# Early gates on 384 tokens, another order of loads and pacing, and seven products for the last block, in an attention and SwiGLU kernel

## The chip, the cores and the metric

The kernel runs on one core of one Trainium2 chip. Its time is the device time of one execution in microseconds (us); where several executions are given, the median is the figure that counts. The profile covers one execution, taken by the hardware profiler; its span runs from the first to the last instruction of the core. The engines are PE (TensorE: matrix products and transposes), ACT (ScalarE), DVE (VectorE), POOL (GpSimd) and SP (SyncE, which only issues transfers here). A tile name such as `kn` or `pg` is the name that the kernel gives to a buffer.

## The reference

Attention over 8 batches, 8 heads, 576 positions and 64 elements per head, causal, with a window of 128 positions and a linear bias that depends on the head; then a gated feed-forward layer over all 8 × 576 = 4608 rows of 512.

```python
scores = scale * np.matmul(q, k.transpose(0, 1, 3, 2))
bias = slopes[:, None, None] * (-np.abs(rel).astype(np.float32))[None, :, :]
mask = (rel >= 0) & (rel < window)                      # window = 128
attn = softmax(np.where(mask, scores + bias[None], -1e9))
x = np.matmul(attn, v)                                  # to 4608 x 512
g = x @ w_gate                                          # 512 x 1536
val = x @ w_val                                         # 512 x 1536
out = (g * (1.0 / (1.0 + np.exp(-g))) * val) @ w_out    # 1536 x 512, out in f32
```

Inputs and output are f32 in HBM; inside, the products run on f16 operands with f32 sums.

## The kernel before

**Tiling.** The attention is cut into 36 units of 128 query rows. A "rank" r = 9 s + p counts them: s is one of four pairs of batches, p = 0 to 7 are the full tiles of the pair, and p = 8 takes the two rests of 64 rows. For each rank there is a load of k, of q and of v (128 KB each). Four consecutive tiles of a batch fill one block of 512 tokens of the feed-forward layer; so there are nine blocks, block 8 being made of the rests.

**Loads.** All of k, q, v and the weights come over POOL's queue, cast from f32 to f16 on the way, in an order written out by hand near the end of the kernel (`load_qk`, `load_v`, `load`, `load_w`; L624 to L646). The two weights of the feed-forward layer come in four column slices each (0 to 256, 256 to 512, 512 to 1024, 1024 to 1536), `wo_sb` in two halves behind rank 8. k and q land in a pool of five buffers each (`kn`, `qn`), and the next load into a buffer waits until it has been transposed. Ranks below 11 are transposed by PE (`transposed`, L201, result `pt`, then copied to `kT` and `qT`); later ones by transfers that SP issues (`transpose`).

**Attention.** `scores` multiplies q and k into `ps` (or `psc` for the tiles with combined masks), ACT takes the exponential (`ex`, `exc`), DVE multiplies by a mask that holds the bias and the window. `reg` (`m_reg`) is the usual mask, made at the start by eight exponentials on ACT; `msk` (`m_c`) are three more, made from it by the four copies of `make_masks` (L109 to L112), and first used by the tile p = 7. `weighted` multiplies by v into `av` and divides by the sum of the weights (`x`), `x_transposed` puts x into `xT` by PE (`px`).

**Feed-forward.** For each block n and each of the 12 slices m of 128 columns, `wide` makes `pg` (gate) and `pv` (value), four matmuls of 512 columns each (L368); ACT takes a tanh (`tt`, L379), DVE makes `uu` = (tt + 1) · pg (L381) and then `hT` = uu · pv (L385). The factor 0.5 that this leaves is put back when the projection is evacuated. `project` is the plain product of `hT` with `wo_sb` (12 matmuls of 512 columns for each of the four groups of 128 rows, L398). `strassen` does it for two groups of rows at a time with seven products of half size, 6 matmuls of 256 columns each (L477), which need sums of the weights (`T1` to `T4`, made by `weight_sums` while block 1 is worked on) and of `hT` (`sums`, four DVE instructions for each of the last three m). Block 0 is projected by `project`, blocks 1 to 7 by `strassen`, block 8 by `project` for three groups of rows and by `last_project` for the fourth, which splits its columns in two halves.

**Order.** `first_tiles` works on tiles 0 to 3 in an order written by hand on PE, DVE and ACT (`tc.manual_schedule`), and begins the gates and values of block 0 on the first 256 or 384 tokens (`begin`, which leaves an open sum in `early`; `wide` finishes it). `everything` then goes through the steps of the generator `ffn`, still by hand up to step 8 (`ALONE`); behind that, a scheduler sets each engine's order from the order in which the program issues its work. How many steps of `attention` are issued between two steps of `ffn` comes from `target`:

```python
target = base + max(0, step - ALONE) + max(0, step - 16) * (32 - b1 + ALONE) / (b1 - 16)
```

With `b1` = 24 the last factor is 2. Block 1 begins at step 24.

**PSUM.** `ps_f` has three buffers `gv` (gates and values) and one `po`; `ps_a` has four buffers, shared by scores, `av`, `px`, `pt`, the gates and values of m = 0 and 1 of block 0, and the projection of block 8.

Of the kernel before, what the change touches and what calls it, by code (L numbers as in the profile page):

```python
# [10 lines left out]
FP32 = mybir.dt.float32  # L11
# [6 lines left out]
WIN = 128  # L18
QK_DMA_FROM = 11
X_DMA_FROM = 24  # L20
ALONE = 8
MANUAL = "compute"
ET = mybir.EngineType
# [23 lines left out]
def kernel(  # L47
# [312 lines left out]
    def wide(n, m, which, c1=512):  # L360

        w, ms = wg_sb if which == "g" else wv_sb, slice(m * P, (m + 1) * P)
        ps, c0 = early.pop((n, m, which), (None, 0))
        if ps is None:
            pool, tag = (ps_a, "a") if (n, m, which) in OTHER else (ps_f, "gv")
            ps = pool.tile([P, 512], FP32, name="p" + which, tag=tag)
        for kb in range(NKB):
            nc.tensor.matmul(ps[:, c0:c1], w[:, kb, ms], xT[n][:, kb, c0:c1],  # L368
                             start=(kb == 0 and c0 == 0), stop=(kb == NKB - 1 and c1 == 512))
        if c1 < 512:  # L370
            early[(n, m, which)] = (ps, c1)
        return ps

    def gate_val(n, m):
        if n not in hT:
            hT[n] = hpool.tile([P, NMB, 512], FP16, name="hT", tag="hT")
        pg = wide(n, m, "g")
        tt = supool.tile([P, 512], FP16, name="tt", tag="tt")
        nc.scalar.activation(tt, pg, AF.Tanh, scale=0.5)  # L379
        uu = supool.tile([P, 512], FP16, name="uu", tag="uu")  # L380
        nc.vector.scalar_tensor_tensor(out=uu, in0=tt, scalar=one if (n, m) == PIN else 1.0, in1=pg,  # L381
                                       op0=ALU.add, op1=ALU.mult)
        yield
        pv = wide(n, m, "v")
        nc.vector.tensor_mul(hT[n][:, m, :], uu, pv)  # L385
        yield

    def rows_of(n, j):
        if n == 8:
            return [(0, 64, 2 * j * S + 512), (64, 128, (2 * j + 1) * S + 512)]  # L390
        return [(0, 128, n * S + j * P)]

    def project(n, j, pool, tag, bufs):
        po = pool.tile([P, DM], FP32, name="po", tag=tag, bufs=bufs)
        for m0 in range(0, NMB, 4):
            for i in range(m0, m0 + 4):
                m = NMB - 1 - i if n == 0 else i
                nc.tensor.matmul(po, hT[n][:, m, j * P:(j + 1) * P], wo_sb[:, m, :],  # L398
                                 start=(i == 0), stop=(i == NMB - 1))
            if m0 + 4 == NMB:  # L400
                osb = opool.tile([P, DM], FP32, name="osb", tag="osb")
                nc.scalar.mul(osb, po, 0.5)
                for p0, p1, r0 in rows_of(n, j):
                    nc.sync.dma_start(out[r0:r0 + p1 - p0, :], osb[p0:p1, :])
            yield

    def last_project(n, j):

        osb = opool.tile([P, DM], FP32, name="osb", tag="osb")
        for half in range(2):  # L410
            c = slice(half * DM // 2, (half + 1) * DM // 2)
            po = ps_a.tile([P, DM // 2], FP32, name="po", tag="a", bufs=4)
            for m in range(NMB):
                nc.tensor.matmul(po, hT[n][:, m, j * P:(j + 1) * P], wo_sb[:, m, c],
                                 start=(m == 0), stop=(m == NMB - 1))
            if half == 0:
                nc.scalar.mul(osb[:, c], po, 0.5)
            else:
                nc.vector.tensor_scalar_mul(osb[:, c], po, 0.5)
            for i, (p0, p1, r0) in enumerate(rows_of(n, j)):  # L420
                (nc.sync if i == 0 else nc.scalar).dma_start(out[r0:r0 + p1 - p0, c], osb[p0:p1, c])
            yield 1.5

# [37 lines left out]
    def strassen(n, t):  # L461

        h = hT[n]
        A11, A12 = h[:, 0:HM, 0:256], h[:, HM:NMB, 0:256]
        S1, A22 = h[:, 0:HM, 256:512], h[:, HM:NMB, 256:512]
        S2, S3, S4 = hsum[n]
        cols = slice(t * P, (t + 1) * P)
        po = ps_f.tile([P, 2, HC], FP32, name="po", tag="po", bufs=1)
        p2 = ps_a.tile([P, HC], FP32, name="p2", tag="a")
        top, low = (opool.tile([P, DM], FP32, name="osb", tag="osb") for _ in range(2))  # L470
        p1s = supool.tile([P, HC], FP32, name="p1s", tag="p1s", bufs=1)
        p5s = supool.tile([P, HC], FP32, name="p5s", tag="p5s", bufs=1)
        u2s = supool.tile([P, HC], FP32, name="u2s", tag="u2s", bufs=1)

        def product(dst, a, b, start=False):
            for m in range(HM):
                nc.tensor.matmul(dst, a[:, m, cols], b[:, m, :], start=(start and m == 0),  # L477
                                 stop=(m == HM - 1), skip_group_check=True)

        def half_plus(dst, a, b):  # L480
            nc.vector.scalar_tensor_tensor(out=dst, in0=a, scalar=0.5, in1=b,
                                           op0=ALU.mult, op1=ALU.add)

        X, Y = po[:, 0, :], po[:, 1, :]
        product(X, A11, B11, True)
# [12 lines left out]
        half_plus(low[:, HC:DM], X, p5s)  # L498
        yield
        product(Y, S4, B22)  # L500
        half_plus(top[:, HC:DM], Y, u2s)
        yield
        product(X, A22, T4)
        nc.scalar.mul(low[:, 0:HC], X, 0.5)
        for j, osb in ((t, top), (t + 2, low)):
            for p0, p1, r0 in rows_of(n, j):
                nc.sync.dma_start(out[r0:r0 + p1 - p0, :], osb[p0:p1, :])
        yield

    AT = {2, 3, *range(5, 10), *range(11, 18)}
# [1 line left out]
    def ffn():  # L514

        for n in range(NBLK):
            if n > 1:
                parts = chain(strassen(n - 1, 0), strassen(n - 1, 1))
            if n == 1:
                for j in range(PRE):  # L520
                    for _ in project(0, j, ps_f, "po", 1):
                        yield 1.0
            for m in range(NMB):
                for half, _ in enumerate(gate_val(n, m)):
                    yield 1.0
                    if n > 1 and 2 * m + half in AT:
                        next(parts)
                        yield 0.75
                if n == 1:
                    if m % 2 and PRE + m // 2 < 4:  # L530
                        for _ in project(0, PRE + m // 2, ps_f, "po", 1):
                            yield 1.0
                    if m in (2, 4, 6):
                        weight_sums(m // 2 - 1)
                if 0 < n < NBLK - 1 and m >= 9:
                    sums(n, m - 9)
            if n > 1:
                assert next(parts, None) is None
        for j in range(3):
            for _ in project(NBLK - 1, j, ps_a, "a", 4):  # L540
                yield 1.0
        yield from last_project(NBLK - 1, 3)


    loaded = done_t = 0
# [31 lines left out]
    def first_tiles():  # L577

        first_masks()
        transposes_to(need[0] + 1)  # L580
        for n, _ in enumerate(run(scores(0))):
            if n == 0:
                transposes_to(need[1])
        for i in range(FIRST):
            if i + 1 < FIRST:
                for n, _ in enumerate(run(scores(i + 1))):
                    if n == 0 and i + 2 < FIRST:
                        transposes_to(need[i + 2])
            weighted(i)

            if i >= 2:
                begin(4, i - 1)
            if i > 0:
                x_transposed(i - 1)
        begin(6, 2)
        begin(4, 3)
        x_transposed(FIRST - 1)
        begin(6, 3)

    def attention():  # L600
# [35 lines left out]
    load_qk(5, "q")  # L636
    load_w(512, 1024)
    load_qk(5, "k")
    load_v(5)
    load_w(1024, 1536)  # L640
    load(6)
    load(7)
    load(8)
    loaded = 9
# [22 lines left out]
    def everything():  # L667
# [3 lines left out]
        with tc.manual_schedule(engines=ENGINES[MANUAL]):  # L671
# [3 lines left out]
            while (at := next(steps)) < ALONE:  # L675
                if at == 2.0:
                    nc.scalar.copy(idm2, idm)
                if at == 5.0:
                    make_masks()
        for step in steps:  # L680

            b1 = 24 + 3 * PRE

# [2 lines left out]
                   else min(NBLK - 1, 2 + int((step + lead - 60) // 34.5)))  # L686
            if step < b1:

                target = base + max(0, step - ALONE) + max(0, step - 16) * (32 - b1 + ALONE) / (b1 - 16)
            elif step < 60:  # L690
                target = base + 32 + SECOND * 8 * (step - b1) / (60 - b1)
            else:
# [35 lines left out]
```

The softmax here doesn't subtract the row's maximum and nothing guards it: scores larger than these inputs give would overflow.

## Time and profile before

| | |
|---|---|
| median of 10 executions | 357.31 us (357.18 to 357.73) |
| profiled execution | 357.18 us |
| its span | 355.4 us, so 1.8 us lie around it |
| mean granted clock of TensorE | 0.998 |
| PE busy | 341.6 us, 96% |
| DVE busy | 272.9 us, 77% |
| ACT busy | 178.2 us, 50% |
| POOL busy | 106.7 us, 30% |

A page of the profile gives the busy time of the engines, then the span in 40 equal slices of some 8.9 us with the busy share in tenths, then the queues of transfers, the chain of work that ended last, and the costliest groups of instructions. A group's line has the source line, the engine, the operation, output and inputs by their names, partitions × elements, the count, busy time and mean duration. A timeline's line has the start, the duration of the group and its operation; in brackets stands how long the engine idled just before it, and what ended that. The matmuls' ends are modelled and overlap with the next start, so spacing, not the single duration, gives their cost.

### The profile page before, as it was taken

Reading aid. Unit: us, or ns where it says so; the run is one execution under the profiler, and the core shown is the slowest. Engines: PE = TensorE matmul, PEld = TensorE weight load, DVE = VectorE, ACT = ScalarE, POOL = GpSimd, SP = SyncE. Lnnn points to the kernel's source line nnn. Section 1 sums busy time; section 2 is a strip of 40 time slices with the busy share of each in tenths; the row PEclk is TensorE's granted clock in tenths of the full one; section 3 lists DMA queues with packets and bytes.
Section 4 is the critical chain, followed back from the end, with each engine's and each line's share of the span. In section 5 each row is a group of like instructions: output and inputs, shape, how many; then the busy total and the mean of one; then the engine's idle time right before and its main releaser. Section 6 shows DMA issues by size and latency. Waiting matters only on the chain.

```text
span 355.4 us, 7251 instructions
## 1 busy us (share of the span) xinstructions
PE 341.6 (96%) x2765; PEld 196.9 (55%) x2765; DVE 272.9 (77%) x595; ACT 178.2 (50%) x353; POOL 106.7 (30%) x132
## 2 busy tenths in 40 slices
PE   7898899999999999999999999999999999999995
PEld 4683454544456655565456655664666566556643
DVE  4858786997977799678986998789878965975540
ACT  4847585555555554555555555455444323332321
POOL 8964755444738354454400100000000000000000
PEclk9999999999999999999999999999999999999999
DMA  9999999999999999999996413311022101101114
GB/s 151 171 186 188 142 172 154 92 148 134 151 139 161 159 157 157 172 145 172 181 75 105 62 59 30 90 31 59 17 75 52 53 2 59 62 0 62 38 43 97
DMA packets 157763, 37.34 MB, mean 105 GB/s; under 512 B 147232, under 2 KB 153248, under 8 KB 157728
## 3 DMA queue, kind: packets, MB, share of 16 engines
q0 software_dynamic: 116224, 18.62, 82.1%
q1 hardware_dynamic: 41056, 17.97, 27.5%
q8 instruction: 21, 0.34, 0.4%
q10 hardware_dynamic: 448, 0.30, 0.3%
q14 instruction: 14, 0.11, 0.1%
HBM read 37.91 MB, written 9.44 MB: 133 GB/s over the span
## 4 chain that ended last, share of the span: by engine, by line
PE 74%; DVE 13%; ACT 5%; DMA 5%; issue 2%; POOL 0%; DVEq 0%; ACTq 0%
PE pg L368 21%; PE pv L368 21%; PE po L477 14%; PE av L319 4%; DMA qn<-in_q_dram 4%; PE ps L254 3%; PE po L398 3%; DVE hT L385 2%; DVE uu L381 2%; PE p L477 2%; DVE ex L263 2%; PE px L345 2%; ACT ex L259 2%; ACT exc L286 1%; PE pt L201 1%
## 5 line engine op out<-in xcount | busy, mean ns | idle before, releaser
L368 PE MATMUL pg<-xT,wg_sb 128*128 128x512 f16 (+2 forms) x464 | 116.4, 365 | 0.2 <-ACT xT L346 0.2
L368 PE MATMUL pv<-xT,wv_sb 128*128 128x512 f16 (+2 forms) x464 | 114.7, 365 | 1.6 <-DVE uu L381 1.6
L379 ACT ACTIVATE tt<-pg 128x512 f16<-128x512 f32 x108 | 65.1, 604 | 85.9 <-PE pg L368 82.5
L381 DVE SCALAR_TENSOR_TENSOR uu<-tt,pg 128x512 f16<-128x512 f16 x107 | 73.2, 684 | 38.0 <-ACT tt L379 37.6
L385 DVE TENSOR_TENSOR hT<-uu,pv 128x512 f16<-128x512 f16 x108 | 73.9, 684 | 6.1 <-PE pv L368 2.1
L368 PEld LDWEIGHTS <-wv_sb 128*128 128x128 f16 x464 | 42.7, 98 | 38.8 <-issue 3.1
L368 PEld LDWEIGHTS <-wg_sb 128*128 128x128 f16 x464 | 42.4, 98 | 35.1 <-issue 2.9
L259 ACT ACTIVATE ex<-ps 128x512 f16<-128x512 f32 x96 | 50.1, 606 | 9.9 <-PE ps L254 9.8
L168 POOL DMA_DIRECT2D va<-in_v_dram x40 | 34.1, 856 | 51.5 <-PE av L319 36.1
L174 POOL DMA_DIRECT2D qn<-in_q_dram x39 | 33.6, 863 | 26.4 <-DMA qT<-qn 20.0
L174 POOL DMA_DIRECT2D kn<-in_k_dram x39 | 33.2, 861 | 26.3 <-DMA kT<-kn 16.1
L477 PEld LDWEIGHTS <-hT 128*128 128x128 f16 x336 | 31.8, 98 | 15.4 <-issue 3.5
L263 DVE TENSOR_TENSOR ex<-ex,m_reg 128x1024 f16<-128x1024 f16 x48 | 32.6, 688 | 8.3 <-ACT ex L259 8.3
L477 PEld LDWEIGHTS <-S 128*128 128x128 f16 x252 | 23.9, 98 | 11.7 <-issue 2.9
L322 DVE TENSOR_TENSOR x<-av,rec 128x256 f16<-128x256 f32 x72 | 29.0, 421 | 0.6
L477 PE MATMUL po<-T,S 128*128 128x256 f16 x168 | 23.0, 273 | 0.6 <-ACT p5s L495 0.6
L477 PE MATMUL po<-T,hT 128*128 128x256 f16 x168 | 23.1, 272 | 0.4
L286 ACT ACTIVATE exc<-psc 128x512 f16<-128x512 f32 x40 | 21.5, 610 | 3.4 <-PE psc L282 3.4
L346 ACT COPY xT<-px 128x512 f16<-128x512 f16 x24 | 14.1, 586 | 15.4 <-PE px L345 15.3
L319 PEld LDWEIGHTS <-ex 128*128 128x128 f16 x384 | 18.3, 97 | 4.9 <-issue 0.7
L319 PE MATMUL av<-va,ex 128*128 128x65 f16 x384 | 20.4, 193 | 0.5
L398 PE MATMUL po<-wo_sb,hT 128*128 128x512 f16 x84 | 19.7, 379 | 0.0
(74 smaller groups left out, 290.0 us busy)
## 6 DMA issues: line engine op xcount, KB each, us to landing
out_dram<-osb SPq DMA_DIRECT2D x32, 256.0 KB, 2.4
va<-in_v_dram POOLq DMA_DIRECT2D x32, 128.0 KB, 8.5
qn<-in_q_dram POOLq DMA_DIRECT2D x31, 128.0 KB, 8.7
kn<-in_k_dram POOLq DMA_DIRECT2D x31, 128.0 KB, 8.1
wo_sb<-in_moe_w_out_dram POOLq DMA_DIRECT2D x2, 768.0 KB, 9.2
wg_sb<-in_moe_w_gate_dram POOLq DMA_DIRECT2D x2, 512.0 KB, 10.8
wv_sb<-in_moe_w_val_dram POOLq DMA_DIRECT2D x2, 512.0 KB, 11.9
out_dram<-osb SPq DMA_DIRECT2D x6, 128.0 KB, 2.4
```

The costliest lines, as they stand in the source:

```text
L168: nc.gpsimd.dma_start(va[rank][p0:p1, :, 0:D], src)
L174: nc.gpsimd.dma_start(t_[p0:p1], src)
L259: nc.scalar.activation(e[:, o:o + 2, :], banks[q4][par], AF.Exp, scale=scale)
L263: nc.vector.tensor_mul(e[:, o, :], e[:, o, :], reg[:, o, :])
L319: nc.tensor.matmul(av[:, j, :], w, val, start=(n == 0), stop=(n == len(todo) - 1))
L322: nc.vector.tensor_mul(x[:, 4 * half:4 * half + 4, :], av[:, :, 0:D], rec.broadcast_to([P, 4, D]))
L368: nc.tensor.matmul(ps[:, c0:c1], w[:, kb, ms], xT[n][:, kb, c0:c1], start=(kb == 0 and c0 == 0), stop=(kb == NKB - 1 and c1 == 512))
L379: nc.scalar.activation(tt, pg, AF.Tanh, scale=0.5)
L381: nc.vector.scalar_tensor_tensor(out=uu, in0=tt, scalar=one if (n, m) == PIN else 1.0, in1=pg, op0=ALU.add, op1=ALU.mult)
L385: nc.vector.tensor_mul(hT[n][:, m, :], uu, pv)
L398: nc.tensor.matmul(po, hT[n][:, m, j * P:(j + 1) * P], wo_sb[:, m, :], start=(i == 0), stop=(i == NMB - 1))
L477: nc.tensor.matmul(dst, a[:, m, cols], b[:, m, :], start=(start and m == 0), stop=(m == HM - 1), skip_group_check=True)
```

## The change

Five things change.

1. In `first_tiles` the gates and values of m = 0 and 1 of block 0 are evacuated for the first 384 tokens around the transposes of the fourth tile, and the last 128 tokens later. For that `gate_val` is split in `gate` and `val`, which take a range of columns.
2. On POOL's queue the loads of k and q of rank 6 go ahead of the load of v of rank 5 and the last slices of the gate and value weights; v of rank 6 stays behind them.
3. `make_masks` is called at step 18 of `ffn`, in the part that the scheduler orders, instead of at step 5 of the part ordered by hand.
4. `target` rises by 1.5 a step from step 8 and by another 1 from step 16, instead of by 1 and by another 2. It is the same at step 24.
5. Block 8 is projected by `strassen` too: its two pairs of groups of rows take turns, product by product. The second pair has its own buffers in PSUM and in the output pool; some stores go out in halves and over ACT's queue as well as SP's, and the last evacuation of each pair is on DVE. `sums` therefore also runs for block 8, and `last_project` goes.

```diff
@@ wide @@
-                             start=(kb == 0 and c0 == 0), stop=(kb == NKB - 1 and c1 == 512))
+                             start=(kb == 0 and c0 == 0), stop=(kb == NKB - 1 and c1 == 512),
+                             skip_group_check=(n == 0))
@@ gate_val @@
+    acted = {}
+
+    def gate(n, m, pg, c0=0, c1=512):
+        if (n, m) not in acted:
+            acted[(n, m)] = [supool.tile([P, 512], FP16, name=i, tag=i) for i in ("tt", "uu")]
+        tt, uu = (t_[:, c0:c1] for t_ in acted[(n, m)])
+        nc.scalar.activation(tt, pg[:, c0:c1], AF.Tanh, scale=0.5)
+        nc.vector.scalar_tensor_tensor(out=uu, in0=tt, scalar=one if (n, m) == PIN else 1.0,
+                                       in1=pg[:, c0:c1], op0=ALU.add, op1=ALU.mult)
+
+    def val(n, m, pv, c0=0, c1=512):
...
+        nc.vector.tensor_mul(hT[n][:, m, c0:c1], acted[(n, m)][1][:, c0:c1], pv[:, c0:c1])
+
+    def gate_val(n, m):
+        c0 = 384 if (n, m) in acted else 0
+        gate(n, m, wide(n, m, "g"), c0)
+        yield
+        val(n, m, wide(n, m, "v"), c0)
         yield
@@ stores @@
+    def store(n, j, osb, c0=0, c1=512, two=False):
+        for i, (p0, p1, r0) in enumerate(rows_of(n, j)):
+            (nc.scalar if two and i else nc.sync).dma_start(out[r0:r0 + p1 - p0, c0:c1],
+                                                            osb[p0:p1, c0:c1])
@@ strassen @@
-        po = ps_f.tile([P, 2, HC], FP32, name="po", tag="po", bufs=1)
+        end = n == NBLK - 1
+        pool, tag, bufs = (ps_a, "a", 4) if end and t else (ps_f, "po", 1)
+        po = pool.tile([P, 2, HC], FP32, name="po", tag=tag, bufs=bufs)
...
         half_plus(low[:, HC:DM], X, p5s)
+        if end and t:
+            store(n, t + 2, low, HC, DM, True)
         yield
         product(Y, S4, B22)
         half_plus(top[:, HC:DM], Y, u2s)
+        store(n, t, top, 0, DM, end)
         yield
         product(X, A22, T4)
-        nc.scalar.mul(low[:, 0:HC], X, 0.5)
...
+        if end:
+            nc.vector.tensor_scalar_mul(low[:, 0:HC], X, 0.5)
+        else:
+            nc.scalar.mul(low[:, 0:HC], X, 0.5)
+        store(n, t + 2, low, 0, HC if end and t else DM, end)
         yield
@@ ffn @@
-                if 0 < n < NBLK - 1 and m >= 9:
+                if n > 0 and m >= 9:
                     sums(n, m - 9)
...
-        for j in range(3):
-            for _ in project(NBLK - 1, j, ps_a, "a", 4):
-                yield 1.0
-        yield from last_project(NBLK - 1, 3)
+        ends = [strassen(NBLK - 1, t) for t in range(2)]
+        for t in 7 * (0, 1):
+            next(ends[t])
+            yield 0.75
@@ first_tiles @@
         begin(4, 3)
+        gate(0, 0, early[(0, 0, "g")][0], 0, 384)
         x_transposed(FIRST - 1)
+        val(0, 0, early[(0, 0, "v")][0], 0, 384)
+        gate(0, 1, early[(0, 1, "g")][0], 0, 384)
+        val(0, 1, early[(0, 1, "v")][0], 0, 384)
         begin(6, 3)
@@ loads @@
     load_qk(5, "k")
+    load_qk(6)
     load_v(5)
     load_w(1024, 1536)
-    load(6)
+    load_v(6)
     load(7)
@@ everything @@
-                if at == 5.0:
-                    make_masks()
         for step in steps:
+            if step == MASKS_AT:
+                make_masks()
...
-                target = base + max(0, step - ALONE) + max(0, step - 16) * (32 - b1 + ALONE) / (b1 - 16)
+                target = base + 1.5 * max(0, step - ALONE) + max(0, step - 16)
```

`MASKS_AT` is 18.0.

More of the change, by code (lines that the diff above doesn't have):

```diff
@@ L20 @@
 X_DMA_FROM = 24
+MASKS_AT = 18.0
 ALONE = 8
@@ L372, in wide @@
         return ps
-    def gate_val(n, m):
+    acted = {}
[7 more added lines that the diff above has]
+    def val(n, m, pv, c0=0, c1=512):
         if n not in hT:
             hT[n] = hpool.tile([P, NMB, 512], FP16, name="hT", tag="hT")
[L377 to L382, printed above, removed]
+        nc.vector.tensor_mul(hT[n][:, m, c0:c1], acted[(n, m)][1][:, c0:c1], pv[:, c0:c1])
+    def gate_val(n, m):
+        c0 = 384 if (n, m) in acted else 0
+        gate(n, m, wide(n, m, "g"), c0)
         yield
-        pv = wide(n, m, "v")
-        nc.vector.tensor_mul(hT[n][:, m, :], uu, pv)
+        val(n, m, wide(n, m, "v"), c0)
         yield
@@ L402, in project @@
                 nc.scalar.mul(osb, po, 0.5)
-                for p0, p1, r0 in rows_of(n, j):
-                    nc.sync.dma_start(out[r0:r0 + p1 - p0, :], osb[p0:p1, :])
+                store(n, j, osb)
             yield
[L407 to L422, printed above, removed]
     HM = NMB // 2
@@ L467, in strassen @@
         cols = slice(t * P, (t + 1) * P)
-        po = ps_f.tile([P, 2, HC], FP32, name="po", tag="po", bufs=1)
+        end = n == NBLK - 1
+        pool, tag, bufs = (ps_a, "a", 4) if end and t else (ps_f, "po", 1)
+        po = pool.tile([P, 2, HC], FP32, name="po", tag=tag, bufs=bufs)
         p2 = ps_a.tile([P, HC], FP32, name="p2", tag="a")
         top, low = (opool.tile([P, DM], FP32, name="osb", tag="osb") for _ in range(2))
-        p1s = supool.tile([P, HC], FP32, name="p1s", tag="p1s", bufs=1)
-        p5s = supool.tile([P, HC], FP32, name="p5s", tag="p5s", bufs=1)
-        u2s = supool.tile([P, HC], FP32, name="u2s", tag="u2s", bufs=1)
+        if end and t:
+            spare = [opool.tile([P, DM], FP32, name="osb", tag="osb") for _ in range(2)]
+            p1s, p5s, u2s = spare[0][:, 0:HC], spare[0][:, HC:DM], spare[1][:, 0:HC]
+        else:
+            p1s, p5s, u2s = (supool.tile([P, HC], FP32, name=i, tag=i, bufs=1)
+                             for i in ("p1s", "p5s", "u2s"))
         def product(dst, a, b, start=False):
@@ L498, in strassen @@
         half_plus(low[:, HC:DM], X, p5s)
+        if end and t:
+            store(n, t + 2, low, HC, DM, True)
         yield
@@ L501, in strassen @@
         half_plus(top[:, HC:DM], Y, u2s)
+        store(n, t, top, 0, DM, end)
         yield
         product(X, A22, T4)
-        nc.scalar.mul(low[:, 0:HC], X, 0.5)
-        for j, osb in ((t, top), (t + 2, low)):
-            for p0, p1, r0 in rows_of(n, j):
-                nc.sync.dma_start(out[r0:r0 + p1 - p0, :], osb[p0:p1, :])
+        if end:
+            nc.vector.tensor_scalar_mul(low[:, 0:HC], X, 0.5)
+        else:
+            nc.scalar.mul(low[:, 0:HC], X, 0.5)
+        store(n, t + 2, low, 0, HC if end and t else DM, end)
         yield
```

## The prediction

> **What bounds the kernel now.** I read the page first. Its top line and its slices say that TensorE sets the time almost everywhere, and that the transfers are saturated in the first half.
>
> ```profile
> PE 341.6 (96%) x2765; PEld 196.9 (55%) x2765; DVE 272.9 (77%) x595; ACT 178.2 (50%) x353; POOL 106.7 (30%) x132
> PE   7898899999999999999999999999999999999995
> DMA  9999999999999999999996413311022101101114
> PE 74%; DVE 13%; ACT 5%; DMA 5%; issue 2%; POOL 0%; DVEq 0%; ACTq 0%
> ```
>
> PE is busy for 341.6 of 355.4 us. What isn't, is in slices 1 to 4 (0 to 36 us) and the last one. The change works at both places, so I looked there next. First the early one, in the timeline (start, duration, operation, in brackets the idle time before it and what ended it):
>
> ```profile
> 26.29 0.63 ACT L109 COPY m_c<-m_reg 128x512 f16<-128x512 f16 x1
> ...
> 28.94 1.04 PE L368 MATMUL pv<-xT,wv_sb 128*128 128x512 f16 x4 [1.15 <-DVE uu L381]
> ...
> 35.35 1.02 PE L368 MATMUL pv<-xT,wv_sb 128*128 128x512 f16 x4 [0.17 <-DVE uu L381]
> ...
> 37.59 0.40 PE L201 MATMUL pt<-idm,qn 128*128 128x128 f16 x4 [0.99 <-DMA qn<-in_q_dram]
> ```
>
> The mask copies hold ACT from 26.29 to 28.57, a tanh stands behind them, its `uu` behind that, and the value product waits 1.15. At 37.59 the transposes of q6 wait 0.99 for their load. With 0.23 (at 24.23, for `xT`), 0.21 (at 27.41) and the 0.17 above, the waits here are 0.23 + 0.21 + 1.15 + 0.17 + 0.99 = **2.75 us**: all that the early part can give. Further on in the timeline of PE:
>
> ```profile
> 54.87 1.89 PE L398 MATMUL po<-wo_sb,hT 128*128 128x512 f16 x8
> ...
> 57.79 0.22 PE L201 MATMUL pt<-idm,kn 128*128 128x128 f16 x1
> 57.98 1.02 PE L368 MATMUL pg<-xT,wg_sb 128*128 128x512 f16 x4
> ...
> 62.29 0.33 PE L201 MATMUL pt<-idm,kn 128*128 128x128 f16 x3
> 62.46 0.61 PE L201 MATMUL pt<-idm,qn 128*128 128x128 f16 x8
> ```
>
> Here block 0's first projection (12 matmuls `po`, 54.87 to 57.95) fills PE before the first gate of block 1 (57.98), and the transposes of k9, q9 and q10 mostly come later (62.29, 62.46). Why this matters is in the DMA view of the issues at 46.2 to 47.1 us:
>
> ```profile
> qn<-in_q_dram POOLq DMA_DIRECT2D x1, 128.0 KB, 12.3
> ```
>
> The load of q10 is issued at 46.32 and lands at 46.32 + 12.3 = **58.6**. By the same reading k9 lands at 53.6, q9 at 54.6 and k10 at 57.7. The tail, from the timeline:
>
> ```profile
> 340.94 7.93 PE L398 MATMUL po<-wo_sb,hT 128*128 128x512 f16 x36
> 348.71 2.78 PE L414 MATMUL po<-wo_sb,hT 128*128 128x256 f16 x24
> 351.53 0.42 DVE L419 TENSOR_SCALAR osb<-po 128x256 f32<-128x256 f32 x1 [9.08 <-PE po L414]
> ```
>
> From 341.1 (end of the last `pv`) to 351.5 PE does nothing but the last block's projection, 10.4 us, and 3.9 us follow to the span's end for the last evacuation and its store.
>
> **What the Trainium skill says.** "DMA: Bandwidth & Descriptors" (Specifications) wants transfers of at least 512 B for line rate; rows of q, k and v are 256 B in f32, and the page of before counts 147232 of 157763 packets under 512 B. It agrees with a queue whose backlog makes a 128 KB load take 12.3 us (8.7 as the page's median), and that means that a reordering moves landings only inside the queue. "TensorE: Matmul & The Clock Gate" (Part 1) says that the array's clock halves after an idle window of some 3.4 us, with free-running windows, and needs a busy window to come back. The trace agrees in kind: the last matmul ends at 351.5, and the granted clock is 1.00 up to 354.0, then
>
> ```profile
> 354.00:354.50 0.50, 0.00 (x0) 0.00 (x0) 0.00 (x0) 0.00 (x0) 0.00 (x0) 0.66 0.00 0
> 354.50:355.00 0.50, 0.00 (x0) 0.00 (x0) 0.00 (x0) 0.00 (x0) 0.00 (x0) 0.50 0.00 0
> ```
>
> (the last three numbers are clock, DMA share, GB/s): some 2.7 us of idleness were enough. "PSUM — Partial Sum Buffer" (PSUM bank collisions) forbids two engines in one bank at once, which bears on the split gates; no row of before shows such a wait.
>
> **The change part by part.**
>
> *Gates on 384 tokens* (`gate`/`val` in `first_tiles`). tanh, `uu` and `hT` of m = 0 and 1 become two pieces, 384 and 128 columns: 6 more instructions on ACT and DVE, while neither is what PE waits for except at 28.94. The new wait: the last 128 columns' matmuls share a bank with what DVE reads, so they stand behind `uu` and `hT` of the first 384. Queued behind them are the other gates and the k5, q5 transposes. Not shown before; bounds 0 and 0.9 us (384/512 of a `uu` and an `hT` at 684 ns each), and I take 0.1 to 0.4, inside what the masks give back.
>
> *Masks later.* In the changed kernel's order the four copies stand on ACT right behind the eight exponentials of the mask, not late at all: ACT waits there for PE's first scores (idle 7.21 to 9.38), and 4 × 0.6 = 2.4 us end about 0.1 late. So this costs at most 0.1 and frees 2.3 us at 26.3; `pv` at 28.94 moves to about 27.7.
>
> *Loads.* k6 and q6 pass v5 and the last W slices on the POOL queue. From the spacing of landings, one 128 KB load per 1 us and 512 KB per 2.4: q6 lands at about 31.7 instead of 37.5, so the 0.99 goes; v5 comes at 32.6 (2 later), the W slices at 35.0 and 37.5 (2 later), wanted by gate and value at about 37; bounds 0 and 0.5. All that follows v6 keeps its place: q10 still lands at 58.6. On SP nothing moves that PE waits for soon.
>
> *Pacing* (`target`). The new order on PE before the first gate of block 1 is: `av`, `px`, k9's four transposes, q9's, q10's four, then `pg`; the 12 `po` come only behind the gates and values of m = 0 and 1. So a wait takes the place of a cover. PE, up to 2.75 early, ends the `av` at about 52.1, waits for k9 (53.6), for q9 (54.6), and then, with nothing else in front, from 55.0 to **58.6** for q10. In-order on PE everything stands behind it, and so do tanh and `uu` of block 1. The early gain is spent in this wait, whether it was 2 or 3.
>
> Then `pg` of block 1 starts at about 58.9, after four transposes and the copy's issue: +0.9 against 57.98. Still undone are 12 `po` × 0.216 (7.77 us for 36) = +2.6; already done are 11 transposes, the rows 0.33 and 0.61 overlapping, −0.6. **Sum +2.9.** What comes back: from 58 to 94 PE was busy 35.3 of 36 us; 0.7 is what a DVE that is now ahead (its weight sums come earlier, it was busy 4.00 of each 4 us from 62 to 78) can give. Bounds 0 and 1.6 (DVE's waits not counted as PE's idleness). I take 0.7, so **+2.2**, carried on a bound PE to the end.
>
> *Last block by seven products.* Removed: 36 matmuls of 512 columns and 24 of 256, 7.77 + 2.63 = 10.40. Added: 14 products × 6 = 84 of 256 columns, at 2.63/24 = 0.1096 each, 9.2 us. −1.2. The sums of block 8 on DVE (12 instructions) lie under the gates of m = 9 to 11, where DVE had waits of 1.65 and 0.25 in the last gates; the last `hT` moves by under 0.2. Stores: the final half is 128x256 again on DVE (0.42), but two rows' stores are near it; 0 to 0.3. I take **−1.1**, bounds −1.4 and 0.
>
> Together +2.2 − 1.1 = +1.1 on a profiled execution of 357.18 (span 355.4 and 1.8 around it): 358.3. The median of the ten runs, 357.31, is 0.13 above it: 358.4, and **358.5** with 0.1 for the split gates.
>
> **The rivals.**
>
> *Faster: q10 is no obstacle.* If the queue's landing drifts earlier with the earlier frees of buffers, or the cover proves larger, the early 2.75 comes through to the end: 357.3 − 2.75 − 1.1 = 353.5. It decides in full when q10 lands before about 55.9 (58.6 − 2.7); the sign turns already when it lands 1.2 earlier than I say, at 57.4, since every us of the wait is one of the sum. For it: less waiting lets POOL issue sooner. Against: DMA slices of 9 up to slice 21 say that the queue, not the issue, sets the landing. A half-way case, q10 at 57.0, gives 358.5 − 1.6 = 356.9.
>
> *Slower: the clock drops in the wait.* From 52.1 to 58.6 PE would have some 0.9 us of work; 2.7 idle us were enough at the end. At half rate for up to one window (3.4 us) from 58.6, the loss is 0 to 1.7, by chance of the window; 359.3 to 360.1. It decides if the record shows a clock under 0.9 between 57 and 62.
>
> *Slower: DVE gives nothing back and the tail gains nothing* (in-order sums in front of `uu`, three `gv` buffers): 357.3 + 2.9 = 360.2, with some tail gain 359.
>
> **How the numbers follow.** A chance of 0.15 for the faster rival, half-way cases with it; 0.45 for the forecast's 358.5 ± 0.8; 0.30 for the clock; 0.10 for the last. About 0.2% (0.7 us) is what a measurement of this kernel can tell from no change. Of the forecast 0.2 lies within it; with 0.02 of the rivals 0.22 same; 0.15 faster; 0.63 slower. The range leaves out the fully faster case and the highest end of the slow ones: 355.6 to 360.4.
>
> **What would show it.** In the profile after: no mask copies at 26; the wait of 0.99 for q6 gone; a wait of PE of some 3.6 us for `qn` ended near 58.6, followed by `pg` of block 1 at 58.9; the first `po` not before 62; the clock in 57 to 62; 84 `po` and `p` matmuls after the last `pv`, in about 9.2 us without a gap. I am wrong if the first gate of block 1 starts before 57.5, if no wait for q10 is there, or if the tail from the last `pv` to the end isn't 0.8 to 1.4 shorter.

## The result, and the profile after

The changed kernel takes 362.44 us (median of 8 executions, 360.75 to 363.36; a ninth on record, 359.79, is not among them) against 357.28 (29 executions) before: a ratio of 1.0138, 95% interval 1.0128 to 1.0149. It is **5.2 us slower**, outside my range, which ended at 360.4. Its executions also spread over 2.6 us, where those of before spread over 0.8. The profiled one is among the short ones: 361.40 us, span 359.6, that is 4.2 more span than before.

The page of the changed kernel, the top line and two lines of slices:

```profile
PE 342.2 (95%) x2789; PEld 200.2 (56%) x2789; DVE 280.8 (78%) x618; ACT 178.8 (50%) x357; POOL 106.7 (30%) x132
PE   7889995999999999999999999999999999999994
PEclk9999998999999999999999999999999999999999
```

The fourth and fifth slices have filled up from 8 to 9 (the third fell from 9 to 8), but the seventh, 54 to 63 us, has fallen from 9 to 5, and it is the only one in which the granted clock is not 9. The timeline of PE there, with start, duration, operation, and in brackets the idle time before it and what ended it:

```profile
52.39 1.03 PE L369 MATMUL pv<-xT,wv_sb 128*128 128x512 f16 x4
54.21 0.29 PE L346 MATMUL px<-idm,x 128*128 128x128 f16 x2 [0.79 <-DVE x L323]
55.41 0.40 PE L202 MATMUL pt<-idm,kn 128*128 128x128 f16 x4 [0.92 <-DMA kn<-in_k_dram]
56.21 0.23 PE L202 MATMUL pt<-idm,qn 128*128 128x128 f16 x1 [0.40 <-DMA qn<-in_q_dram]
...
58.92 0.61 PE L202 MATMUL pt<-idm,qn 128*128 128x128 f16 x4 [2.20 <-DMA qn<-in_q_dram]
59.32 1.91 PE L369 MATMUL pg<-xT,wg_sb 128*128 128x512 f16 x4
61.02 1.40 PE L369 MATMUL pv<-xT,wv_sb 128*128 128x512 f16 x4
62.26 1.03 PE L369 MATMUL pg<-xT,wg_sb 128*128 128x512 f16 x4
...
63.99 2.75 PE L415 MATMUL po<-wo_sb,hT 128*128 128x512 f16 x12
```

Four waits stand in a row: for x on DVE, for k9, for q9 and, 2.20 long, for q10, which lands at 58.9. They make 4.3 us; between them PE does eight transposes and two pairs of `px`. Then the first gate of block 1 takes 1.91 instead of 1.02: it runs at half the clock. The windows of the same kernel say when (the number third from the end is the clock):

```profile
57.00:58.00 1.00, 0.00 (x0) 0.00 (x0) 0.77 (x2) 0.17 (x1) 1.00 (x2) 1.00 2.43 154
58.00:59.00 1.00, 0.08 (x2) 0.09 (x2) 0.00 (x0) 0.00 (x0) 1.00 (x2) 0.68 2.52 159
59.00:60.00 1.00, 1.00 (x6) 0.62 (x7) 0.42 (x1) 0.00 (x0) 1.00 (x2) 0.50 2.42 152
60.00:61.00 1.00, 1.00 (x3) 0.30 (x2) 0.00 (x0) 0.00 (x0) 0.44 (x2) 0.50 2.46 154
61.00:62.00 1.00, 1.00 (x4) 0.40 (x3) 0.10 (x1) 0.60 (x1) 0.63 (x1) 0.61 2.55 153
```

The four gates and values from 59.32 to 63.99 take 4.67 us; the four of before, from 57.98 to 61.43, took 3.45. So the clock cost 1.2 here. At the end of the last `pv` (341.10 before, 345.51 after) the kernel is 4.4 late, and it was 4.4 late at the `av` of 71.55 (67.15 before): in the 270 us between nothing came back. The end of the chain of work that ended last:

```profile
344.63 0.88 PE pv L369 x4
345.51 1.31 PE po L481 x12
346.82 1.31 PE p L481 x12
348.13 6.70 PE po L481 x60
...
354.85 0.42 DVE osb L512
```

PE's last stretch is 9.32 us instead of 10.40, without a wait. But from its end to the end of the span it is 4.77 us instead of 3.90, and the DMA view of the last stores, issued at 355.5 on SP and ACT, says why:

```profile
out_dram<-osb SPq DMA_DIRECT2D x1, 64.0 KB, 2.8
out_dram<-osb ACTq DMA_DIRECT2D x1, 64.0 KB, 2.9
```

Before, the last two, issued at 352, landed sooner after their issue:

```profile
out_dram<-osb SPq DMA_DIRECT2D x1, 64.0 KB, 2.0
out_dram<-osb ACTq DMA_DIRECT2D x1, 64.0 KB, 2.2
```

The span's balance is 4.41 − 1.08 + 0.87 = 4.2.

### The profile page after: what moved, and what is told of

Same layout as the page of the kernel before. It is cut to its first block, busy times and chain, and to the rows that moved or that the text cites. A ratio compares the mean times of both kernels' runs of the same rounds, so it can differ in the third digit from the quotient of the medians.

```text
span 359.6 us, 7334 instructions
## 1 busy us (share of the span) xinstructions
PE 342.2 (95%) x2789; PEld 200.2 (56%) x2789; DVE 280.8 (78%) x618; ACT 178.8 (50%) x357; POOL 106.7 (30%) x132
## 4 chain that ended last, share of the span: by engine, by line
PE 75%; DVE 9%; DMA 6%; ACT 5%; issue 2%; POOL 1%; DVEq 0%; ACTq 0%; POOLq 0%
PE pv L369 21%; PE pg L369 21%; PE po L481 16%; PE av L320 4%; DMA qn<-in_q_dram 3%; PE ps L255 3%; DMA va<-in_v_dram 3%; PE p L481 3%; PE po L415 2%; DVE hT L391 2%; DVE ex L264 2%; DVE uu L384 2%; ACT ex L260 2%; PE px L346 2%; ACT tt L383 1%
## 5 line engine op out<-in xcount | busy, mean ns | idle before, releaser
L383 ACT ACTIVATE tt<-pg 128x512 f16<-128x512 f32 (+2 forms) x110 | 65.7, 597 | 86.5 <-PE pg L369 83.0
L384 DVE SCALAR_TENSOR_TENSOR uu<-tt,pg 128x512 f16<-128x512 f16 (+2 forms) x109 | 73.5, 674 | 33.2 <-ACT tt L383 32.6
L391 DVE TENSOR_TENSOR hT<-uu,pv 128x512 f16<-128x512 f16 (+2 forms) x110 | 74.2, 674 | 6.6 <-PE pv L369 1.9
L481 PEld LDWEIGHTS <-hT 128*128 128x128 f16 x384 | 36.4, 98 | 16.3 <-issue 3.5
L481 PEld LDWEIGHTS <-S 128*128 128x128 f16 x288 | 27.4, 98 | 12.3 <-issue 2.9
L481 PE MATMUL po<-T,S 128*128 128x256 f16 x192 | 26.0, 273 | 0.6 <-ACT p5s L499 0.6
L481 PE MATMUL po<-T,hT 128*128 128x256 f16 x192 | 26.1, 272 | 0.5
L255 PE MATMUL ps<-qT,kT 64*128 64x256 f16 x192 | 17.2, 272 | 1.4 <-DVE qT L207 0.8
```

What stands on the lines that cost most here:

```text
L255: nc.tensor.matmul(two[par][:, j, :], kT[rows, ks, pair, :], qT[rows, p:p + 2, pair, :], start=(j == 0), stop=(j == 1))
L383: nc.scalar.activation(tt, pg[:, c0:c1], AF.Tanh, scale=0.5)
L391: nc.vector.tensor_mul(hT[n][:, m, c0:c1], acted[(n, m)][1][:, c0:c1], pv[:, c0:c1])
```

## The experiments

The theory after this reading: q10's landing holds the first gate of block 1, the clock falls in the wait, the 12 `po` that used to cover the time are still to be done, and the seven products gain nothing because the stores bunch. The rivals: the new gates or the later v5 and weight slices cost the time; the missing cover costs by itself; the seven products cost it. In all that follows, a time without "profiled" is a median, and its ratio is to the kernel before on the same chip. The runs come from several chips, so two of them are best compared by these ratios; 0.001 is 0.36 us.

### The order of before, with all the rest (old_pacing)

```diff
-                target = base + 1.5 * max(0, step - ALONE) + max(0, step - 16)
+                target = base + max(0, step - ALONE) + max(0, step - 16) * (32 - b1 + ALONE) / (b1 - 16)
```

> Only the pacing formula goes back to the one of before; gates, loads, masks and tail stay as changed. On PE the 12 po matmuls of block 0 stand before the first gate of block 1 again, q10's transposes behind it. Theory (the order in front of block 1 costs PE the q10 wait, with a clock drop in it): no wait for qn near 58, clock 1.00 in 57 to 62, first gate of block 1 at 55.3 to 56.5 instead of 59.3, time 354.5 to 356. Rival (the split gates, or the later v5 and W slices, cost the time): stays near 362. Rival (the early 2.75 us can't come through): 357.

Measured: **355.99 us**, ratio 0.9966 (0.9954 to 0.9979), clock 1.00 from 57 to 65. Its timeline of PE:

```profile
53.63 1.89 PE L415 MATMUL po<-wo_sb,hT 128*128 128x512 f16 x8
...
56.74 1.02 PE L369 MATMUL pg<-xT,wg_sb 128*128 128x512 f16 x4
```

The `po` stand in front again, no load is waited for, and block 1 begins 1.24 earlier than before. One formula decides between 5.2 us of loss and 1.3 of gain; the gates, loads and masks don't cause the loss. I had put 354.5 at the lower end: the early gain is 1.2 us, not 2.75.

### The same order of instructions, another landing (qk_first)

```diff
     loaded = 9
+    load_qk(9)
+    load_qk(10)
     for a0 in (0, 6):
...
-            load(loaded)
+            load_v(loaded) if loaded in (9, 10) else load(loaded)
```

> The changed kernel with the loads of k and q of ranks 9 and 10 moved ahead of both halves of wo on POOL's queue; the order of instructions on PE and DVE is that of the changed kernel, instruction for instruction. Theory (the landing of q10 is the cause, not the order in itself): q10 lands near 48 to 50, PE does not wait for k9, q9 or q10, clock 1.00, the first gate of block 1 at 53.5 to 54.5, and the time is 353.5 to 356 although 12 po matmuls still stand behind block 1's first gates. Rival (the missing cover of po costs by itself, or DVE holds block 1): 358 or more. A third outcome: wo, which lands later (56 to 58), is waited for by the weight sums on DVE or by po.

(The first half of this edit stands ahead of the two halves of `wo_sb`.) Measured: **356.85 us**, ratio 0.9998 (0.9989 to 1.0006). PE, DVE and ACT execute the changed kernel's instructions in its order; POOL's queue differs. The load of q10 is issued at 43.3 instead of 46.6, and the two loads of q issued there (42.4 and 43.3) land a median of 4.0 us later, where q10 took 12.3:

```profile
54.09 0.29 PE L346 MATMUL px<-idm,x 128*128 128x128 f16 x2 [0.79 <-DVE x L323]
...
54.60 0.55 PE L202 MATMUL pt<-idm,qn 128*128 128x128 f16 x7
55.76 1.02 PE L369 MATMUL pg<-xT,wg_sb 128*128 128x512 f16 x4 [0.60 <-ACT xT L347]
...
59.21 2.75 PE L415 MATMUL po<-wo_sb,hT 128*128 128x512 f16 x12
```

No load is waited for there and the clock stays up. Against the changed kernel the first gate starts 3.6 earlier (55.76, 59.32) and the `po` 4.8 earlier (59.21, 63.99), the rest being the clock. By the two ratios, 1.0138 and 0.9998, **some 5.0 us is what the late landing costs**, the clock's fall with it: the whole loss. The time is still 0.9 above the 356 that I had expected at most, and the first gate came later too (53.5 to 54.5 expected), because 0.79 for x and 0.60 for `xT` are waits of the new order itself. So this run only equals the kernel before. The rival that the missing cover costs by itself did not come true at its size (358 or more), but it is not nothing: pre1 below, which has the cover, is faster than this run by 1.6 us by the ratios.

### One load less ahead of q10 (q10_sooner)

```diff
-            load(loaded)
+            if loaded == 9:
+                load_qk(9)
+            elif loaded == 10:
+                load_qk(10)
+                load_v(9)
+                load_v(10)
+            else:
+                load(loaded)
```

> The changed kernel with v of rank 9 loaded behind q of rank 10, so that one load of 128 KB less stands ahead of k10 and q10; orders on PE and DVE as in the changed kernel. Theory: q10 lands about 1 us sooner, near 57.7, the wait falls to about 1.2, and the idle stretch is short enough in most executions that the clock does not drop or drops later: time 362.4 minus 1 for the landing, minus up to 1.5 for the clock: 359.9 to 361.4. Rival (the wait is not what decides): unchanged, 362.4.

Measured: 359.34 us, ratio 1.0073 (1.0056 to 1.0089), by the ratios 2.3 below the changed kernel; it is 0.6 below what I had expected at best. In its profiled execution q10 lands at 56.8 and PE waits 0.21 for it:

```profile
56.78 0.40 PE L202 MATMUL pt<-idm,qn 128*128 128x128 f16 x4 [0.21 <-DMA qn<-in_q_dram]
```

How much of this is the landing can't be read: that execution was already 1.5 us behind the changed kernel's profiled one at 26 us, after a wait of 1.03 for the first q (0.58 at most in the other profiles) and a half clock near 10 us (0.59 over 8 to 12), which the other profiles do not show. The direction agrees with the theory; the amount stays open.

### The cover put in by the program (pre1)

```diff
-PRE = 0
+PRE = 1
```

> The changed kernel with PRE = 1: the first group of rows of block 0 is projected ahead of block 1 by the program's own order, so that 12 po matmuls and then two gates, two values and 12 more po stand in front of q10's transposes. Theory: no wait over 1 us between 52 and 62, clock 1.00, the first gate of block 1 at about 55.5, time 354 to 356. Rival (something else than q10 holds PE there, such as DVE or ACT): a wait of another kind takes its place and it stays above 358.

`PRE` is the number of groups of rows of block 0 that the program projects ahead of block 1; with 1, the step `b1` at which block 1 begins moves from 24 to 27. Measured: **355.51 us**, ratio 0.9953 (0.9938 to 0.9968). On PE 12 `po`, the first gate of block 1, three more gates and values, 12 more `po`, and only then q9 and q10:

```profile
53.42 1.89 PE L415 MATMUL po<-wo_sb,hT 128*128 128x512 f16 x8
...
56.52 1.02 PE L369 MATMUL pg<-xT,wg_sb 128*128 128x512 f16 x4
...
59.98 2.75 PE L415 MATMUL po<-wo_sb,hT 128*128 128x512 f16 x12
...
62.73 0.61 PE L202 MATMUL pt<-idm,qn 128*128 128x128 f16 x8
```

From 36 to 100 us its timeline of PE shows one wait, 0.32 at 51.85, and further on none above 0.36. The gate came 1 later than I expected, again for the smaller early gain.

### The tail alone, and all but the tail (tail_only, early_only)

The first is the kernel before with part 5 of the change and nothing else, the second the changed kernel with the old projection of block 8.

> The kernel before with the last block by seven products and nothing else of the change. Theory (PE gains 1.1, the stores bunched at the end take 0.9 of it back): 0.0 to 0.4 us faster than before, 356.9 to 357.3; from the last evacuation's start to the end of the span 4.7 us instead of 3.9. Rival (the loss at the end comes with the early part, not from the seven products): 1.1 faster, 356.2.

> The changed kernel with the last block projected as before (36 matmuls of 512 columns and 24 of 256). Theory: the whole loss is early, so the wait for q10 and the clock drop are as in the changed kernel and the time is its 362.4 plus 0.0 to 0.4. Rival (the seven products are what slows it): 357 to 358.

Measured: tail_only **357.12 us**, ratio 0.9999 (0.9991 to 1.0007); early_only **361.66 us**, ratio 1.0119 (1.0105 to 1.0133). The loss is early, all of it. In tail_only PE ends at 350.09 instead of 351.50, and 5.0 us follow instead of 3.9 (I had expected 4.7), since the last two stores land 3.0 and 3.2 us after their issue:

```profile
350.11 0.42 DVE L512 TENSOR_SCALAR osb<-po 128x256 f32<-128x256 f32 x1 [0.23 <-PE po L481]
```

What PE saves, the stores take. early_only measured 0.7 below the changed kernel by the ratios, where I had 0 to 0.4 above; the changed kernel's spread (360.75 to 363.36) is wider than that.

### The changed kernel once more (after_again)

> The changed kernel itself, profiled once more. Theory (the clock's windows run freely, so where they fall on the wait differs between executions): the same wait of about 2.2 us for q10, within 0.2, but another moment and length of the half clock in 57 to 63 and so another time, within 360.7 to 363.4. Rival (the spread comes from the transfers): the landing of q10 differs by 1 us or more and the half clock does not.

Measured: two executions, 361.05 and 362.07 us, with mean clocks of 0.994 and 0.990. The profiled one waits 2.19 for q10 (2.20 in the first profile); q10 lands 0.8 sooner than there (58.1, 58.9), and PE is there sooner by as much, so the rival's 1 us is not reached. Its half clock lies from about 57.8 to 61.2; in the first it is from about 58.4 to 61.8. The moment differs, as I had expected, the length doesn't: both are 3.4 us long. In early_only, with the wait again at 2.21 (from 56.07 to 58.28), it lasts from about 56.2 to 63.1, twice as long, and its four gates and values take 64.31 − 58.69 = 5.62 us, 2.2 more than at full clock. Its windows in steps of 3.41 us (PE's busy time is the second number, the clock the third from the end):

```profile
52.83:56.24 3.41, 1.31 (x13) 0.68 (x12) 1.91 (x5) 1.17 (x3) 1.94 (x3) 1.00 2.45 152
56.24:59.65 3.41, 1.36 (x7) 0.81 (x8) 1.31 (x3) 0.29 (x1) 3.30 (x4) 0.50 2.45 155
59.65:63.06 3.41, 3.41 (x10) 1.17 (x9) 1.44 (x3) 0.60 (x1) 0.88 (x1) 0.50 2.55 154
```

The clock fell when only 0.2 us of the wait for q10 had passed, behind 3.4 us in which PE had worked for 1.3. In the 3.4 us after the fall PE worked for 1.4, and the clock stayed down; in the next 3.4 it worked without a pause, and the clock came back. In the two profiles of the changed kernel PE worked for 0.9 and 0.5 us of the 3.4 before the fall and for 2.9 and 3.1 of the 3.4 after it, and the clock came back after one such stretch. So the wait is the same each time, and where the fall lies on it decides how long the half clock lasts. That is part of the spread. For the executions without a trace it is only likely: their mean clocks, which the fall at the kernel's end lowers too, lie at 0.990 to 0.991 for six of the changed kernel's eight, but at these alone the times go from 361.91 to 363.36, and this difference stays open.

### What each early part is worth (pre1_nosplit, pre1_oldloads, pre1_oldmasks)

Each is pre1 with one part undone: the evacuation of 384 tokens, the loads of rank 6, the place of the masks.

> PRE = 1 as in the run of that name, without the early evacuation of 384 tokens. Theory (the split exchanges one wait for another: in the changed kernel 0.33 for uu and 0.28 for hT before the last 128 columns): within 0.4 us of PRE = 1, 355.1 to 355.9. Rival (the split is what brings the early gain): 356.3 or more.

> PRE = 1 with the loads of rank 6 in the order of before. Theory (PE waits for q6 again, near 36, and everything behind it on PE is late by that): a wait of 1 to 2.5 us for qn, 356.2 to 357.5. Rival (the wait is taken back before block 1 starts, because something else holds PE there): 355.5.

> PRE = 1 with the four mask copies at step 5 of the part ordered by hand, as before. Theory (2.3 us of ACT in front of a tanh that PE's gates wait for): waits of PE for uu of about 1 us come back near 28 to 30, 356.2 to 356.8. Rival (with the split gates ACT is no longer close to PE's path there): 355.5.

Measured: **356.43** (0.9973, 0.9962 to 0.9984), **360.17** (1.0088, 1.0068 to 1.0107) and **356.32** (0.9969, 0.9957 to 0.9981), against 355.51. Without the split this wait comes back, at the place and with the length that it had before the change:

```profile
28.94 1.04 PE L369 MATMUL pv<-xT,wv_sb 128*128 128x512 f16 x4 [1.15 <-DVE uu L384]
```

So by the medians the split saves 0.9 (the interval overlaps that of pre1 a little); my theory, that it trades one wait for another, was wrong, and the rival right. In this run no mask copy stands in front, so the 1.15 was not theirs, as I had read it from the profile of before. The masks save 0.8 by the medians (again with overlapping intervals), a time in my range, by a wait of 0.51 for `uu` at 30.96 and one for x. The loads are the surprise, in the timeline of PE of pre1_oldloads:

```profile
37.76 0.40 PE L202 MATMUL pt<-idm,qn 128*128 128x128 f16 x4 [3.93 <-DMA qn<-in_q_dram]
```

With the new pacing one gate and one value fewer stand in front, so PE is at q6 by 33.8 (37.76 − 3.93), where before it was 36.6 (37.59 − 0.99), and waits 3.93 instead of 0.99, more than the 2.5 that I had as the most. A half clock follows from 38.5 to 41.9; the 4.7 us are the wait and the clock together. The loads of rank 6 had to move because the pacing was quickened; for ranks 9 and 10 the same step was not taken, and that is the loss of the changed kernel.

### The stores of the tail (pre1_stag, pre1_stores, pre1_spstores)

All three are pre1 with another end. First, fewer turns between the two pairs of rows:

```diff
-        for t in 7 * (0, 1):
+        for t in 2 * (0, 1) + 5 * (0,) + 5 * (1,):
```

> PRE = 1 as in the run of that name, and the two pairs of rows of the last block no longer take turns throughout: two products each in turn, then five of the first pair, then five of the second. Theory (the stores bunch in the last 5 us): the first pair's stores leave some 3 us earlier, from the last evacuation's start to the end of the span 3.9 to 4.2 us instead of 4.8, time 0.6 to 0.9 below PRE = 1 alone, 354.6 to 354.9. Rival (each product now waits for the evacuation of the one before in the same bank): PE's last stretch grows from 9.3 us to 10 or more and the time is that of PRE = 1 or longer.

Measured: 357.03 us, 0.9998 (0.9990 to 1.0006). Behind the last evacuation's start it is 3.9 us instead of 4.8, as expected, but the rival holds: PE's last stretch grows from 9.3 to 12.0 us. With one pair alone, a product has to wait for the evacuation of the product before it, which lies in the same tile `po`:

```profile
344.40 0.81 PE L481 MATMUL po<-T,S 128*128 128x256 f16 x6 [0.31 <-ACT p5s L499]
...
345.79 0.81 PE L481 MATMUL po<-wo_sb,S 128*128 128x256 f16 x6 [0.35 <-DVE osb L485]
...
349.16 0.82 PE L481 MATMUL po<-wo_sb,S 128*128 128x256 f16 x6 [0.57 <-DVE osb L485]
```

Then every half row stored once it is there, on both queues (shown), and the same with the first of them on SP alone (pre1_spstores, without the `True` in the first added call):

```diff
         half_plus(top[:, 0:HC], p2, p1s)
         yield
+        if end:
+            store(n, t, top, 0, HC, True)
...
-        if end and t:
+        if end:
             store(n, t + 2, low, HC, DM, True)
...
-        store(n, t, top, 0, DM, end)
+        store(n, t, top, HC if end else 0, DM, end)
...
-        store(n, t + 2, low, 0, HC if end and t else DM, end)
+        store(n, t + 2, low, 0, HC if end else DM, end)
```

> PRE = 1 with the last block's stores each sent as soon as its half row is evacuated, on SP's and ACT's queues alike; the order of the products stays alternating. Theory (too much of the output leaves at the end): a quarter of the 1 MB goes out 5 us sooner, and from the last evacuation's start to the end of the span it takes 4.0 to 4.3 us instead of 4.8; time 0.5 to 0.8 below PRE = 1, 354.7 to 355.0. Rival (more issues on the two queues delay the last one): 355.5 or more.

> As the run with the stores sent by half rows, but the first quarter (behind the second product) is issued by SP alone, so that ACT has no transfers to issue while evacuations still wait on it. Theory (half rows shorten the last landing; what was lost there was PE's wait of 0.88 for an evacuation behind ACT's two issues): PE's last stretch is 9.3 us without a wait, from the last evacuation's start to the end of the span 4.1 to 4.5 us, time 354.8 to 355.2 where PE's last stretch begins as with PRE = 1. Rival (smaller stores cost by themselves as much as they save): 355.5 or more.

Measured: pre1_stores 356.12 us (0.9970, 0.9958 to 0.9981), pre1_spstores **355.26** (0.9943, 0.9929 to 0.9956). In the first the last stores do land 2.0 us after issue instead of 2.8 and 2.9, and 4.4 us follow the last evacuation's start instead of 4.8; but ACT was issuing when PE needed an evacuation:

```profile
342.36 1.47 ACTq L407 DMA_DIRECT2D out_dram<-osb  x2
343.87 0.38 ACT L498 ACTIVATE u2s<-po 128x256 f32<-128x256 f32 x1 [2.65 <-PE po L481]
...
344.31 0.92 PE L481 MATMUL po<-T,hT 128*128 128x256 f16 x7 [0.88 <-ACT u2s L498]
```

The second has no such wait: PE's last stretch is 9.3 us again. Yet from the last evacuation's start (348.59) to the span's end it takes 5.2 us, not the 4.1 to 4.5 that I expected. The last landing is short (2.0), but ACT's last issue starts only at 350.4, 1.4 us after the data was ready at 349.0, since its six issues take 5.2 us. So large stores bunch in the transfer and small ones in the issue. Its 355.26 is the shortest time of the study, just outside my 354.8 to 355.2, and not told apart from pre1 by the intervals.

## Why the prediction was wrong

The mechanism was the one I named: the block's `po` no longer stands in front, PE waits for q10 (58.9 for my 58.6), block 1 starts at 59.3 (58.9), 12 `po` are undone and 11 transposes done. What failed is the sum. Three of its terms were mis-sized, all to one side: the clock, left out as 0, the 0.7 that were to come back, and the tail's gain of 1.1.

- **The clock.** I kept it as a rival of chance 0.30 and left it out of the sum, although I had the fall at the end of before in front of me. All three profiles with this order and this landing show it. It is priced at 0 to 1.7 in the prediction; the profiles have 1.2 to 1.3 (the changed kernel, twice) and 2.2 (early_only), since the half clock can last 6.8 us and not one window. The Trainium skill's "TensorE: Matmul & The Clock Gate" (Part 1) was the right page, and its window of some 3.4 us, which runs freely, is what the record shows: in every trace the stretches between two changes of the clock are whole multiples of 3.413 us (among them 3.41, 6.83, 34.1, 51.2, 297 and 348). But the page asks for an idle window, and none stood in front: PE had worked for 0.5 to 1.3 of the 3.4 us before these falls.
- **What comes back.** I took −0.7 for 58 to 94. It was 0.1: the gate's 1.34, the `po` less the transposes, 2.0, and the clock's 1.2 make 4.5, and PE was 4.40 late at 71.55 and 4.41 at the last `pv`. The idleness that I had counted on, 0.7 us from that `av` to 94, is almost all still there (0.71 of 26.85 us before, 0.56 of the same stretch after).
- **The tail.** I had −1.2 for PE and −1.1 with the stores, for which I allowed 0.3 at most. PE gave −1.08; the stores took 0.87 back in the profile, so the tail is 0.2 shorter and not 0.8 to 1.4, my own sign of being wrong. tail_only shows no gain.
- **The first gate.** +0.9 predicted, +1.34 measured: 0.3 from the landing, 0.1 from the transposes at half clock. The waits ahead of it were cut otherwise than I had them (2.20 for q10 and not 3.6), since k9 and q9 landed 1.6 to 1.8 later than I had read them from before.
- **The early gain.** 2.75 was the sum of the visible waits, and I said that the wait for q10 would swallow whatever of it there was; it did. It was smaller all the same, 1.24 in old_pacing: the split brought waits of 0.34 for `uu` and 0.27 for `hT` in the shared bank (I had bounded them by 0 and 0.9 and taken 0.1 to 0.4), and x on DVE held PE twice more in old_pacing (0.23 and 0.32) where nothing did before. The Trainium skill's "PSUM — Partial Sum Buffer" (PSUM bank collisions) lets one expect the first two, since two engines must not be in one bank at once.
- **The masks.** I had the 1.15 at 28.94 as the end of a chain that began with their copies. pre1_nosplit has no copies there and the same wait: on DVE `uu` and `hT` follow each other almost without a pause from 25.3 on, in both kernels, and the split is what ends it.

So the sum was +1.1; with 0.4 for the gate, 1.2 for the clock, 0.6 for what did not come back and 0.9 for the stores it is the 4.2 of the profiled span. The median lies 1 us higher, likely by the clock. I had two of the three terms as a rival of their own (360.2) and the clock as another, each alone; that they could come together is what the range left out.

The split gates, masks and loads, on which I spent most terms, are each a gain of 0.8 to 4.7 once the cover is there and the pacing is quickened. The rival "faster" failed at its stated point: q10 did not land before 57.4. That it decides was right: qk_first, where q10 lands before PE is there, is on the level of before, and pre1, which needs no early q10, is faster.

## What to carry to other kernels

When a change makes an engine earlier, list the transfers that it will meet next and their landings: an order that was good enough can put the one transfer that didn't move in front of everything. Independent work that already has its data belongs in front of the wait, by the program's own order if a scheduler can move it; and where TensorE would have little to do for some 3.4 us, add the price of a lower clock and a spread between executions, even if no single wait is that long. Ask also what happens when two rivals come true together. For the last block, count when its outputs become ready, not only how long the products take.

## What the runs showed of the hardware that I had not expected

Away from the end of the kernel, the clock fell to half in five profiles. In the 3.4 us before the fall PE had worked for 0.9, 0.5, 1.3, 0.7 and 1.6 us (the changed kernel twice, early_only, pre1_oldloads, q10_sooner), so no fully idle window was needed. In early_only the fall came 0.2 us into the wait, in pre1_oldloads 0.7 and in q10_sooner 1.9 us after the wait had ended. It lasted 3.4 us in four of them, where PE worked for 2.9 us or more of it, and 6.8 in early_only, where the first 3.4 held 1.4 us of work. In qk_first the leanest 3.4 us in this part held 2.0 us of work and the clock stayed up; where the border lies is not shown.

Issuing one store took ACT 0.55 to 0.78 us in the changed kernel and up to 1.65 in pre1_spstores, and meanwhile it evacuates nothing (PE's wait of 0.88 in pre1_stores); on SP it took 0.33 to 0.57 in the changed kernel.
